# The second early expert slot: weights and x in two parts and three products, split while the first early slot runs

## The chip, the cores and the metric

The kernel runs on one core of one Trainium2 chip. The metric is device time in microseconds (us) of one execution. Inputs are laid out on the host before the launch; everything else is in the one launch that is timed.

## What is computed

The reference chains three parts (numbers: 3072 tokens of 384 features, from 4 batches, 768 steps, 8 heads of 48):

```python
# 1. linear attention with a decaying state
state = f[:, :, t, :, None] * state + einsum('bhd,bhe->bhde', k[:, :, t], v[:, :, t])
y[:, :, t] = einsum('bhd,bhde->bhe', q[:, :, t], state)
# 2. a mixture of 8 experts, one for each token, chosen by the largest logit
h = maximum(x[mask] @ w1[e], 0.0)          # 384 -> 1024
out[mask] = gate_w[mask, None] * (h @ w2[e])   # 1024 -> 384
# 3. a gated unit
out = (sigmoid(x @ w_gate) * (x @ w_val)) @ w_out   # 384 -> 1536 -> 384
```

The change lies in part 2.

## The kernel before, in words

**Stages.** Attention and routing run first, 24 token tiles of 128. Routing gives each token a place in its expert's list; a table of places, built by small matmuls from one-hot rows ("marks"), tells later which tokens an expert slot gathers. A slot is one expert's work on 256 gathered tokens. Two slots are "early": their experts and tokens are known from the first 18 tiles, so they can run while the tables for all other slots are still being made. After them come half slots (128 tokens; two run with these inputs), ten whole slots, and the gated unit, which takes over half of the time.

**A slot's steps.** A slot has eight steps f = 0 to 7, then f = 8 and 9. In a step TensorE makes 128 columns of h for the 256 tokens from three pieces of x and w1 (tile h, 128x256), ScalarE applies relu, and two steps later TensorE multiplies that h by w2 for two groups of 128 tokens (tile y, 128x384). Hooks hang on the steps: other work that is issued, in program order, right after a step's relu. Each engine takes its instructions in that order, so a hook's work on an engine stands ahead of all that the slot issues later on it.

**Two forms of a slot.** `slot32` (L688) keeps weights and x as fp32 and makes each product with one fp32 matmul: three for h (L704), one for each y (L694). VectorE has no part in it. `slot` (L646) holds weights and x as two fp32r parts, hi and lo, and makes three products: hi by hi, hi by lo, lo by hi (L656 to L659 for h, L735 for y). Its h needs the same: ScalarE writes relu(h) as hh (L662), and VectorE subtracts, max(h, 0) - hh, into hl (L663). `split` (L385) makes the parts of a weight piece of 128x1536: a ScalarE copy into hi (L388) and a subtraction into lo (L389), on VectorE or, if asked, on GpSimd. `transpose_x` (L399) turns gathered x with TensorE, copies it into xth with ScalarE (L405) and subtracts into xtl with VectorE (L406); `turn_x` (L723) only turns and copies it.

**The two early slots before.** Both are `slot32`. Their weights, `w0` and `w1`, four pieces each, are loaded together (L1350 to L1354, SyncE's queue). The first slot, `slot_0`, starts in the last attention round (L1284). Its hooks (L1402) are:

- f3: two loads of the weights of the gated unit, then six steps of the slot tables (`tab(6)`, VectorE, up to the expert numbers e_i, L546)
- f4: loads of the next expert's first weights, which wait for e_i; then five more steps of the tables, up to L580
- f5: `lates`, the marks of the last six tiles (VectorE, L307 and L309, six pairs)
- f6: `turn_x` for the second slot
- f7: a weight load
- f9, in the middle of the slot's last y products: `put_table` (L325), where TensorE puts the marks into the table (L331) and VectorE adds them (L334); a weight load

The second slot's hooks (L1429): at f0 `take_ids` (L341, TensorE reads the table; L343, VectorE), the gathers by GpSimd and one table step; f1 the rest of the tables; f2, f4, f5 VectorE work on the weights of the gated unit (`convert_high`, `convert_low`, L850 to L864) and, at f4 and f5, the split of `head`, the first piece of the next slot's weights (L1417, L1418); f8 and f9 `transpose_x` for the next slot. A branch (L1636) on the number of half slots follows it.

Of the kernel before, what the change touches and what calls it, by code (L numbers as in the profile page):

```python
# [45 lines left out]
STAGED = (3, 7)  # L46
# [14 lines left out]
def kernel(  # L61
# [16 lines left out]
    nc = tc.nc  # L78
# [10 lines left out]
    def ctile(shape, dtype, name):  # L89
        return const.tile(shape, dtype, name=name, tag=name)  # L90
# [42 lines left out]
    xth = ctile([P, 3, 256], F32R, "xth")  # L133
    xtl = ctile([P, 3, 256], F32R, "xtl")
    xg = ctile([P, 2, ROW], F32, "xg")
# [238 lines left out]
    st = {}  # L374

    def load_piece(e_reg, j, to=None):
        nc.sync.dma_start(out=raw[j] if to is None else to, in_=w12[bass.ds(e_reg, 1), j].rearrange("o p f -> (o p) f"))

    def alloc_w(pool, pre, j):
        return (  # L380
            pool.tile([P, 1536], F32R, name=f"{pre}h{j}", tag=f"{pre}h{j}"),
            pool.tile([P, 1536], F32R, name=f"{pre}l{j}", tag=f"{pre}l{j}"),
        )

    def split(dst, src, eng=None):  # L385

        hi, lo = dst
        nc.scalar.copy(out=hi, in_=src)  # L388
        (eng or nc.vector).tensor_tensor(out=lo, in0=src, in1=hi, op=ALU.subtract)  # L389
# [9 lines left out]
    def transpose_x(src, hi, lo, ts=(0, 1)):  # L399
        for t in ts:  # L400
            ps = ps_t.tile([P, 3, P], F32, tag="t", name="xT")
            for c in range(3):
                nc.tensor.transpose(ps[:, c, :], src[:, t, c * P:(c + 1) * P], ident)  # L403
            sl = slice(t * P, (t + 1) * P)
            nc.scalar.copy(out=hi[:, :, sl], in_=ps)  # L405
            nc.vector.tensor_tensor(out=lo[:, :, sl], in0=ps, in1=hi[:, :, sl], op=ALU.subtract)  # L406
# [222 lines left out]
    def run(steps):  # L629
        for _ in steps:  # L630
            pass

    def take_cur(src=None, ts=(0, 1)):
        cur = small.tile([P, 2, 2], F32, tag="cur", name="cur")
        sl = slice(0, len(ts))
        nc.gpsimd.tensor_copy(out=cur[:, sl], in_=xg[:, sl, DM:DM + 2] if src is None else src[:, sl])
        return cur
# [8 lines left out]
    def slot(w, hooks, src=None, last=False):  # L646

        cur = st.pop("cur") if "cur" in st else take_cur(src)
        yps = [ps_o.tile([P, DM], F32, tag="o", name=f"y{t}") for t in range(2)]
        hs = {}  # L650
        for f in range(9):
            if f < 8:
                hi, lo = (t.rearrange("p (c n f) -> p c n f", c=3, n=4)[:, :, f % 4, :] for t in w[f // 4])
                ps = ps_mm.tile([P, 256], F32, tag="mm", name="h")
                for c in range(3):
                    nc.tensor.matmul(out=ps, lhsT=hi[:, c, :], rhs=xth[:, c, :], start=(c == 0), stop=False)  # L656
                    nc.tensor.matmul(out=ps, lhsT=hi[:, c, :], rhs=xtl[:, c, :], start=False, stop=False)  # L657
                for c in range(3):
                    nc.tensor.matmul(out=ps, lhsT=lo[:, c, :], rhs=xth[:, c, :], start=False, stop=(c == 2))  # L659
                hh = hp["p"].tile([P, 256], F32R, tag="hh", name="hh", bufs=4)  # L660
                hl = hp["p"].tile([P, 256], F32R, tag="hl", name="hl", bufs=4)
                nc.scalar.activation(out=hh, in_=ps, func=AF.Relu)  # L662
                nc.vector.scalar_tensor_tensor(  # L663
                    out=hl, in0=ps, scalar=0.0, in1=hh, op0=ALU.max, op1=ALU.subtract
                )
                hs[f] = (hh, hl)
            for hook in hooks.get(f, ()):
                hook()
            if 2 <= f < 8:
                for t in range(2):  # L670
                    second_product(hs[f - 2], yps[t], w, f - 2, t)
            yield
        for t in range(2):
            for g in (6, 7):
                second_product(hs[g], yps[t], w, g, t)
            for hook in hooks.get(9, ()) if t == 0 else ():
                hook()
            ysb = hp["p"].tile([P, ROW], F32, tag="ysb", name="ysb", bufs=3)
            if t and last:
                nc.vector.tensor_scalar(  # L680
                    out=ysb[:, 0:DM], in0=yps[t], scalar1=cur[:, t, 0:1], scalar2=None, op0=ALU.mult
                )
            else:
                nc.scalar.activation(out=ysb[:, 0:DM], in_=yps[t], func=AF.Copy, scale=cur[:, t, 0:1])
            nc.gpsimd.tensor_copy(out=ysb[:, DM:ROW], in_=cur[:, t, :])
            st["y", t] = ysb

    def slot32(w, x, hooks, cur):  # L688

        yps = [ps_o.tile([P, DM], F32, tag="o", name=f"y{t}") for t in range(2)]  # L690
        hs = {}

        def second(g, t):
            nc.tensor.matmul(  # L694
                out=yps[t], lhsT=hs[g][:, t * P:(t + 1) * P], rhs=w[2 + g // 4][:, (g % 4) * DM:(g % 4 + 1) * DM],
                start=(g == 0), stop=(g == 7),
            )

        for f in range(9):
            if f < 8:  # L700
                piece = w[f // 4].rearrange("p (c n f) -> p c n f", c=3, n=4)[:, :, f % 4, :]
                ps = ps_mm.tile([P, 256], F32, tag="mm", name="h")
                for c in range(3):
                    nc.tensor.matmul(out=ps, lhsT=piece[:, c, :], rhs=x[:, c, :], start=(c == 0), stop=(c == 2))  # L704
                hs[f] = hp["p"].tile([P, 256], F32, tag="hh", name="h32", bufs=4)
                nc.scalar.activation(out=hs[f], in_=ps, func=AF.Relu)
            for hook in hooks.get(f, ()):
                hook()
            if 2 <= f < 8:
                for t in range(2):  # L710
                    second(f - 2, t)
            yield
        for t in range(2):
            for g in (6, 7):
                second(g, t)
            for hook in hooks.get(9, ()) if t == 0 else ():
                hook()
            ysb = hp["p"].tile([P, ROW], F32, tag="ysb", name="ysb", bufs=3)
            nc.scalar.activation(out=ysb[:, 0:DM], in_=yps[t], func=AF.Copy, scale=cur[:, t, 0:1])
            nc.gpsimd.tensor_copy(out=ysb[:, DM:ROW], in_=cur[:, t, :])  # L720
            st["y", t] = ysb

    def turn_x(x, ts=(0, 1)):  # L723

        for t in ts:
            ps = ps_t.tile([P, 3, P], F32, tag="t", name="xT")
            for c in range(3):
                nc.tensor.transpose(ps[:, c, :], xg[:, t, c * P:(c + 1) * P], ident)
            nc.scalar.copy(out=x[:, :, t * P:(t + 1) * P], in_=ps)
# [84 lines left out]
    stage = {}  # L814
# [415 lines left out]
    pools = {0: (wa, "a")}  # L1230
# [6 lines left out]
    early_x = [raw[2][:, 0:768].rearrange("p (c n) -> p c n", c=3)]  # L1237
    early_cur = []
# [6 lines left out]
    for i in range(NT + 2):  # L1245
# [103 lines left out]
        if i == NE + 2:  # L1349
            w0, w1 = ([wa.tile([P, 1536], F32, name=f"e{h}{j}", tag=f"a{h}{j}") for j in range(4)] for h in "hl")  # L1350
# [20 lines left out]
        stage[j] = staged.tile([P, 1536], F32, name=f"stage{j}", tag=f"stage{j}")  # L1371
    cv = ExitStack()
    hp["cv"] = cv.enter_context(tc.tile_pool(name="cv", bufs=1))
    early_x.append(stage[STAGED[-1]][:, 0:768].rearrange("p (c n) -> p c n", c=3))

    def each(hooks, **more):
        for f, fn in more.items():
            hooks.setdefault(int(f[1:]), []).extend(fn if isinstance(fn, list) else [fn])
        return hooks
# [7 lines left out]
    lates = late_marks()  # L1387

    def tab(n):
        for _ in range(n):  # L1390
            next(tables)
# [5 lines left out]
    def load_first():  # L1397
        st["e0"] = expert(0)
        for x in range(2):
            load_piece(st["e0"], x)  # L1400

    each(  # L1402
        hooks_0,
        f3=[convert_load, convert_load, lambda: tab(6)],
        f4=[load_first, lambda: tab(5)],
        f5=lambda: run(lates), f6=lambda: turn_x(early_x[1]),
        f7=lambda: load_piece(st["e0"], 2),
        f9=[put_table, lambda: load_piece(st["e0"], 3)],
    )
    run(slot_0)  # L1410
# [15 lines left out]
    def load_n():  # L1426
        st["n"] = nc.values_load(tabs["n"][0:1, 0:1], min_val=0, max_val=NHALF)

    run(slot32(w1, early_x[1], each(  # L1429
        {},  # L1430
        f0=[take_ids, lambda: gather_x(NTOK, 0), lambda: tab(1)],
        f1=[lambda: early_y.extend(scatter_y(tabs["edst"][:, 0])), lambda: run(tables)],
# [1 line left out]
        f4=[lambda: part(head, 0, 0), convert_mask, convert_high],  # L1434
        f5=[lambda: part(head, 0, 1), convert_low, convert_store],
        f7=load_n,
        f8=lambda: transpose_x(xg, xth, xtl, (0,)),
        f9=[lambda: transpose_x(xg, xth, xtl, (1,)), lambda: next_x((0, 1), (0, 1), 1)],
    ), early_cur[1]))
    scatter_y(tabs["edst"][:, 1], apart=early_y)  # L1440


# [324 lines left out]
```

## Time and profile before

| | |
|---|---|
| median of 3 runs | 879.07 us (875.2 to 879.09) |
| the profiled execution | 878.71 us |
| its span, first to last instruction | 877.0 us |
| granted TensorE clock, mean over the span | 0.991 |
| TensorE (PE) busy | 853.0 us, 97% |
| VectorE (DVE) busy | 476.8 us, 54% |
| ScalarE (ACT) busy | 389.2 us, 44% |
| GpSimd (POOL) busy | 249.8 us, 28% |

Times in the rows are in microseconds from the start of the span, durations in microseconds too unless marked ns. PE is TensorE, PEld its weight loads, DVE VectorE, ACT ScalarE, POOL GpSimd, SP SyncE; a "q" behind the name is the engine's sequencer. An fp32 matmul is recorded as two MATMUL records, so "x6" are three of them.

### The profile page before, as it was taken

What the parts mean: (1) busy time and instruction counts of PE and PEld (TensorE: products, weight loads), DVE (VectorE), ACT (ScalarE), POOL (GpSimd) and SP (SyncE); (2) the same over time, 40 slices, a digit from 0 to 9 for tenths busy, and PEclk for the clock granted to TensorE, in tenths of its full rate; (3) what the DMA queues carried; (4) which work ended last, traced back from release to release, by engine and by line L of the source; (5) the groups of instructions that cost most, each with busy time, mean ns of one, the idle gap of its engine ahead of it and who ended that gap; (6) DMA issues with size and microseconds to landing.
All of it is one profiled execution on the core that took longest, in us unless ns stands there. A gap on an engine that the chain in (4) does not pass through costs nothing.

```text
span 877.0 us, 15315 instructions
## 1 busy us (share of the span) xinstructions
PE 853.0 (97%) x5802; PEld 762.9 (87%) x5802; DVE 476.8 (54%) x1036; ACT 389.2 (44%) x804; POOL 249.8 (28%) x321
## 2 busy tenths in 40 slices
PE   7999999999999999999999999999999999999995
PEld 6888888777999999999888888888888888888885
DVE  5777778475987979976335334333423433442221
ACT  5866675225866656656432322232322332223222
POOL 5744443113445665564630200020020001002002
PEclk8999999999999999999999999999999999999998
DMA  9566653864989979976202021011012002000000
GB/s 324 177 219 232 217 171 123 332 242 149 336 302 327 330 270 321 333 260 226 80 10 64 27 47 35 1 55 37 18 46 46 19 1 64 10 0 37 1 1 36
DMA packets 52273, 121.15 MB, mean 138 GB/s; under 512 B 21018, under 2 KB 33318, under 8 KB 52192
## 3 DMA queue, kind: packets, MB, share of 16 engines
q1 hardware_dynamic: 47200, 105.10, 35.6%
q0 software_dynamic: 4992, 15.00, 4.8%
q8 instruction: 47, 0.77, 0.4%
q14 instruction: 34, 0.28, 0.1%
HBM read 96.44 MB, written 20.11 MB: 133 GB/s over the span
## 4 chain that ended last, share of the span: by engine, by line
PE 69%; DVE 4%; issue 1%; ACT 1%; POOL 0%; POOLq 0%; DVEq 0%; ACTq 0%
PE gv L1595 11%; PE gv L1596 11%; PE gv L1594 11%; PE y L735 8%; PE o L1619 6%; PE o L1617 6%; PE o L1618 6%; PE h L659 3%; PE h L656 3%; PE h L657 3%; DVE cvt L850 2%; DVE al L389 1%; DVE hl L663 1%; PE xT L403 0%; DVE bl L389 0%
## 5 line engine op out<-in xcount | busy, mean ns | idle before, releaser
L1605 DVE TENSOR_TENSOR sg<-sg,gv 128x256 f32<-128x256 f32 (+1 forms) x145 | 60.2, 415 | 209.3 <-PE gv L1596 209.3
L1606 ACT CAST gh<-sg 128x256 fp32r<-128x256 f32 (+1 forms) x145 | 58.7, 405 | 191.6 <-DVE sg L1605 191.6
L1625 POOL DMA_INDIRECT out_dram<-raw,tok x24 | 23.6, 984 | 375.5 <-ACT raw L1622 369.3
L1607 DVE TENSOR_TENSOR gl<-sg,gh 128x256 fp32r<-128x256 f32 (+1 forms) x145 | 64.3, 443 | 68.2 <-ACT gh L1606 68.2
L1604 ACT ACTIVATE sg<-gv 128x256 f32<-128x256 f32 (+1 forms) x145 | 55.2, 381 | 94.7 <-PE gv L1596 92.6
L393 POOL DMA_INDIRECT xg<-xd,ids x24 | 36.5, 1523 | 62.9 <-PE xT L403 38.9
L662 ACT ACTIVATE hh<-h 128x256 fp32r<-128x256 f32 x80 | 30.9, 386 | 42.7 <-PE h L659 42.0
L663 DVE SCALAR_TENSOR_TENSOR hl<-h,hh 128x256 fp32r<-128x256 f32 x80 | 33.3, 419 | 21.8 <-ACT hh L662 18.2
L1596 PE MATMUL gv<-oddh,al 128*128 128x512 f32 (+1 forms) x120 | 44.3, 369 | 0.0
L1595 PE MATMUL gv<-oddl,ah 128*128 128x512 f32 (+1 forms) x120 | 44.3, 369 | 0.0
L1594 PE MATMUL gv<-oddh,ah 128*128 128x512 f32 (+1 forms) x120 | 44.1, 367 | 0.0
L1596 PE MATMUL gv<-oddh,bl 128*128 128x512 f32 x108 | 42.5, 394 | 0.0
L1596 PE MATMUL gv<-evenh,bl 128*128 128x512 f32 x108 | 42.5, 393 | 0.0
L1595 PE MATMUL gv<-oddl,bh 128*128 128x512 f32 x108 | 42.4, 393 | 0.0
L1595 PE MATMUL gv<-evenl,bh 128*128 128x512 f32 x108 | 42.4, 393 | 0.0
L945 POOL TENSOR_TENSOR qT<-kq,g 128x512 f32<-128x512 f32 x19 | 24.4, 1283 | 62.9 <-ACT g L935 47.8
L1596 PE MATMUL gv<-evenh,al 128*128 128x512 f32 x108 | 42.3, 391 | 0.0
L1595 PE MATMUL gv<-evenl,ah 128*128 128x512 f32 x108 | 42.2, 391 | 0.0
L1594 PE MATMUL gv<-evenh,ah 128*128 128x512 f32 x108 | 42.0, 389 | 0.0
L1594 PE MATMUL gv<-evenh,bh 128*128 128x512 f32 x108 | 42.0, 389 | 0.0
L1594 PE MATMUL gv<-oddh,bh 128*128 128x512 f32 x108 | 42.0, 389 | 0.0
L975 DVE TENSOR_TENSOR am<-a,causal 128x512 f32<-128x512 f32 x48 | 31.2, 683 | 12.5 <-PE a L969 12.5
(365 smaller groups left out, 2487.8 us busy)
## 6 DMA issues: line engine op xcount, KB each, us to landing
raw<-in_w_dram SPq DMA_DIRECT2D x48, 768.0 KB, 5.8
kq<-in_att_kq_dram SPq DMA_DIRECT2D x24, 512.0 KB, 5.4
cvr<-in_w_glu_dram SPq DMA_DIRECT2D x14, 768.0 KB, 7.4
raw<-wd SPq DMA_DIRECT2D x7, 768.0 KB, 5.3
f<-in_att_fv_dram SPq DMA_DIRECT2D x24, 200.0 KB, 5.6
v<-in_att_fv_dram SPq DMA_DIRECT2D x24, 200.0 KB, 2.5
x<-yd SPq DMA_DIRECT2D x12, 386.0 KB, 3.4
xd<-rows SPq DMA_DIRECT2D x5, 772.0 KB
```

Of the source, the lines that this page charges most:

```text
L663: nc.vector.scalar_tensor_tensor(out=hl, in0=ps, scalar=0.0, in1=hh, op0=ALU.max, op1=ALU.subtract)
L735: nc.tensor.matmul(out=ps, lhsT=lhs[:, ts], rhs=rhs[:, fs], start=(g == 0 and part == 0), stop=(g == 7 and part == 2))
L1594: nc.tensor.matmul(out=ps[:, ns], lhsT=hi[:, sl], rhs=xh[:, c, ns], start=(c == 0), stop=False)
L1595: nc.tensor.matmul(out=ps[:, ns], lhsT=hi[:, sl], rhs=xl[:, c, ns], start=False, stop=False)
L1596: nc.tensor.matmul(out=ps[:, ns], lhsT=lo[:, sl], rhs=xh[:, c, ns], start=False, stop=(c == 2))
L1604: nc.scalar.activation(out=sg[:, sl], in_=pss[0][:, to], func=AF.Sigmoid)
L1605: nc.vector.tensor_tensor(out=sg[:, sl], in0=sg[:, sl], in1=pss[1][:, to], op=ALU.mult)
L1606: nc.scalar.copy(out=gh[:, sl], in_=sg[:, sl])
L1607: nc.vector.tensor_tensor(out=gl[:, sl], in0=sg[:, sl], in1=gh[:, sl], op=ALU.subtract)
L1617: nc.tensor.matmul(out=ps, lhsT=gh[:, ts], rhs=hi[:, fs], start=(f == 0), stop=False)
L1618: nc.tensor.matmul(out=ps, lhsT=gh[:, ts], rhs=lo[:, fs], start=False, stop=False)
L1619: nc.tensor.matmul(out=ps, lhsT=gl[:, ts], rhs=hi[:, fs], start=False, stop=(f == 11))
```

## The change

The second early slot becomes a `slot`. New tiles w1s, hi and lo of all four pieces of w1, lie in the pool of the odd slots' weights. They are made by `split` from hooks of the first slot: piece 0 at f3 and piece 2 at f4, with GpSimd subtracting, pieces 1 and 3 at f7 and f8, with VectorE subtracting. x of the second slot is made by `transpose_x` into xth and xtl at f6 in place of `turn_x`. The hooks of the second slot stay as they were.

```diff
-    early_x.append(stage[STAGED[-1]][:, 0:768].rearrange("p (c n) -> p c n", c=3))
...
+    w1s = [alloc_w(*pools[1], j) for j in range(4)]
+
+    def split_early(j, eng=None):
+        split(w1s[j], w1[j], eng)
+
     each(
         hooks_0,
-        f3=[convert_load, convert_load, lambda: tab(6)],
-        f4=[load_first, lambda: tab(5)],
-        f5=lambda: run(lates), f6=lambda: turn_x(early_x[1]),
-        f7=lambda: load_piece(st["e0"], 2),
+        f3=[convert_load, convert_load, lambda: split_early(0, nc.gpsimd), lambda: tab(6)],
+        f4=[load_first, lambda: split_early(2, nc.gpsimd), lambda: tab(5)],
+        f5=lambda: run(lates), f6=lambda: transpose_x(xg, xth, xtl),
+        f7=[lambda: load_piece(st["e0"], 2), lambda: split_early(1)],
+        f8=lambda: split_early(3),
         f9=[put_table, lambda: load_piece(st["e0"], 3)],
     )
     run(slot_0)
...
-    run(slot32(w1, early_x[1], each(
+    st["cur"] = early_cur[1]
+    run(slot(w1s, each(
         {},
         f0=[take_ids, lambda: gather_x(NTOK, 0), lambda: tab(1)],
...
-    ), early_cur[1]))
+    )))
     scatter_y(tabs["edst"][:, 1], apart=early_y)
```

## Rows read from the trace of the kernel before

**Rows 1.** The page's first part: busy time, share, instructions of each engine.

```profile
PE 853.0 (97%) x5802; PEld 762.9 (87%) x5802; DVE 476.8 (54%) x1036; ACT 389.2 (44%) x804; POOL 249.8 (28%) x321
```

**Rows 2.** Windows, second early slot (length; busy of PE, PEld, DVE, ACT, POOL).

```profile
188.98:212.02 23.04, 22.28 (x92) 16.21 (x90) 13.12 (x30) 8.73 (x17) 7.92 (x10) 1.00 0.35 117
```

**Rows 3.** Timeline, PE, from the end of the first early slot (start, duration).

```profile
187.96 1.51 PE L694 MATMUL y<-eh,h 128*128 128x384 f32 x4
...
190.60 0.55 PE L341 MATMUL take<-sel,table 96*128 96x52 f32 x4
...
212.02 0.39 PE L753 MATMUL h<-head,xth 128*128 128x256 f32 x1 [0.76 <-ACTq L1636]
```

**Rows 4.** Timeline, PE, one step of the second early slot (fp32).

```profile
196.22 1.45 PE L694 MATMUL y<-el,h 128*128 128x384 f32 x4
...
198.81 1.45 PE L694 MATMUL y<-el,h 128*128 128x384 f32 x4
```

**Rows 5.** Timeline, PE, one step of a later slot (three fp32r products).

```profile
296.34 0.34 PE L735 MATMUL y<-ah,hh 128*128 128x384 f32 x1
...
298.45 0.34 PE L735 MATMUL y<-ah,hh 128*128 128x384 f32 x1
```

**Rows 6.** By line: splits and xtl of later slots (ns: min/median/max).

```profile
L388 ACT CAST bh<-raw x22: 1463/1473/1491, 236.4 to 406.6; 128x1536 fp32r<-128x1536 f32 x22
L389 DVE TENSOR_TENSOR bl<-raw,bh x17: 1745/1747/1759, 237.9 to 408.1; 128x1536 fp32r<-128x1536 f32 x17
L389 POOL TENSOR_TENSOR bl<-raw,bh x5: 3499/3648/3696, 264.5 to 410.7; 128x1536 fp32r<-128x1536 f32 x5
L406 DVE TENSOR_TENSOR xtl<-xT,xth x23: 545/547/559, 208.9 to 398.7; 128x384 fp32r<-128x384 f32 x23
```

**Rows 7.** Timeline, DVE, in the two early slots.

```profile
175.08 0.25 DVE L506 TENSOR_REDUCE blocks<-fcmp 128x8 f32<-128x96 f32 x1
175.37 0.17 DVE L509 TENSOR_TENSOR blocks<-tiles,blocks 128x8 f32<-128x8 f32 x1
...
187.21 0.30 DVE L309 TENSOR_SCALAR raw<-iota_lo,late_lo,iota_t 128x128 f16<-128x128 bf16 x1
188.16 0.42 DVE L334 TENSOR_TENSOR table<-table,put 96x256 f32<-96x256 f32 x1 [0.65 <-PE put L331]
...
191.18 0.21 DVE L343 TENSOR_SCALAR ids<-take 128x52 int32<-128x52 f32 x1 [2.61 <-PE take L341]
```

**Rows 8.** Timeline, ACT, relus of steps 3 and 4 of the first early slot.

```profile
172.90 0.38 ACT L706 ACTIVATE h<-h 128x256 f32<-128x256 f32 x1 [2.67 <-PE h L704]
176.56 0.38 ACT L706 ACTIVATE h<-h 128x256 f32<-128x256 f32 x1 [3.27 <-PE h L704]
```

**Rows 9.** Timeline, SyncE's and POOL's queues in the two early slots.

```profile
181.22 7.26 SPq L377 DMA_DIRECT2D raw<-in_w_dram  x4
192.19 1.02 POOL L393 DMA_INDIRECT xg<-xd,ids  x1 [20.30 <-DVE skip L594]
```

**Rows 10.** Timeline, DVE and POOL at once, in three places.

```profile
143.70 1.33 DVE L309 TENSOR_SCALAR place<-iota_lo,lo,iota_t 128x128 f16<-128x128 bf16 x1
143.71 1.27 POOL L945 TENSOR_TENSOR qT<-kq,g 128x512 f32<-128x512 f32 x1 [4.75 <-ACT g L935]
...
251.19 3.52 POOL L389 TENSOR_TENSOR al<-raw,ah 128x1536 fp32r<-128x1536 f32 x1
251.72 4.61 DVE L389 TENSOR_TENSOR al<-raw,ah 128x1536 fp32r<-128x1536 f32 x1 [2.12 <-ACT ah L388]
...
264.45 3.50 POOL L389 TENSOR_TENSOR bl<-raw,bh 128x1536 fp32r<-128x1536 f32 x1 [4.25 <-ACT bh L388]
265.14 0.42 DVE L663 SCALAR_TENSOR_TENSOR hl<-h,hh 128x256 fp32r<-128x256 f32 x1 [0.50 <-ACT hh L662]
```

**Rows 11.** Timeline, PE, a wait in a later slot.

```profile
256.71 0.44 PE L735 MATMUL y<-ah,hl 128*128 128x384 f32 x1 [1.84 <-DVE hl L663]
```

**Rows 12.** Windows, just behind that wait (PE clock third from the end).

```profile
257.60:261.00 3.40, 3.40 (x16) 3.40 (x15) 3.37 (x6) 0.86 (x2) 2.43 (x3) 0.53 0.84 292
```

## Prediction

> **What bounds the kernel now.** I read the page first: TensorE is busy for 97% of the span [rows 1], so a change pays where it shortens TensorE's own work, and only while nothing else makes TensorE wait. Then the windows: in the second early slot TensorE works 22.28 of 23.04 us, VectorE 13.12 and ScalarE 8.73 [rows 2]. That slot is bound by TensorE, and its fp32 form asks nothing of VectorE. Then the timeline of TensorE around the seam: the first slot's last y products start at 187.96, behind `put_table`; `take_ids` runs at 190.60; the slot ends at 212.02 - 0.76 = 211.26, and after the branch the next slot starts at 212.02 [rows 3]. Last the timeline of VectorE: its tables and marks run with no gap worth naming until the last mark, 187.21 + 0.30 = 187.51, and it then waits 0.65 for TensorE before it adds the table at 188.16 [rows 7]. That row is the one to see: VectorE is less than a microsecond from being the bound at this place.
>
> **The change, part by part.**
>
> *Second slot, TensorE.* From one y to the next a step lasts 198.81 - 196.22 = 2.59 us in fp32 [rows 4] and 298.45 - 296.34 = 2.11 in three products [rows 5], about half of it h and half y. Eight steps save 8 x 0.48 = 3.8 us. This is all the change can gain.
>
> By the Trainium skill ("FP8 and Floating Point Precision", TensorE Precision Notes) a true fp32 product is four passes through the array; three products of one pass would then save a quarter. A quarter of 8 x 2.59 is an estimated 5.2 us, and the sum below would end 1.4 us lower; the rows show 19%, not 25%, and they decide.
>
> *ScalarE, first slot.* Four copies of 1.47 us [rows 6], and two of x that replace two. ScalarE waits 2.67 and 3.27 us for TensorE before the relus of steps 3 and 4 [rows 8], so I cost them at nothing. Without that cover a relu would be 1.47 late, and the y that needs it comes two steps later.
>
> *GpSimd, first slot.* Two subtractions of about 3.5 us [rows 6]. The first can start after relu and copy, 172.90 + 0.38 + 1.47 = 174.8; the second at 176.56 + 0.38 + 1.47 = 178.4 [rows 8], just as the first ends. Nothing that is urgent queues behind them: GpSimd idles 20.30 us before the gather at 192.19 [rows 9]. But VectorE works at the same time, and that has a price. A TENSOR_TENSOR on VectorE with both inputs in SBUF, 1.75 us alone [rows 6], took 4.61 beside a GpSimd subtraction and ended 1.6 us after it. A mark of L309, 0.30 alone [rows 7], took 1.33 and ended 0.05 us after a GpSimd multiplication. A hl of L663, which reads one input from PSUM, was not held at all, 0.42 [rows 10]. The tables and marks are nearly all of the first kinds. Bounds: nothing, if they behave as L663; 2 x 3.65 = 7.3 us if both subtractions hold VectorE throughout. It can't be a gain, since no work leaves VectorE here. I take 6.7: the two subtractions, 7.0, less the reduction (0.25) that can run under the first [rows 7]; the rows of the marks are the nearest, being the same instruction.
>
> [...]
>
> *SyncE.* The weight loads at 181.22 [rows 9] wait for the expert numbers that VectorE makes, and slide by the same 6.7 us, as do the two loads behind them in the queue. They are first wanted by a hook in the fifth step of the second slot, which slides too, so I cost this at nothing; the next loads start only behind the branch.
>
> *The put.* With the last mark at 187.51 + 6.7 = 194.2, TensorE, which stands at `put_table`, resumes its y at 187.96 + 6.7 = 194.7.
>
> *VectorE, end of the first slot.* Behind the marks come two xtl (2 x 0.55) and two subtractions (2 x 1.75) [rows 6], and only then, in program order, the addition to the table (0.42) [rows 7]: 194.2 + 1.1 + 3.5 + 0.4 = 199.2. TensorE is through its y (half a fp32 step, 1.3) and the first h (1.1) at 197.1 and waits 2.1 us at `take_ids`. Take starts at 199.3 in place of 190.60 [rows 3], 8.7 late.
>
> *VectorE, second slot.* Now each y needs a hl from VectorE, and the hl stand in its queue between the tables and the weight conversions. From the ids on, VectorE has its 13.12 us of the window [rows 2], less two xtl that come at the end (1.1), so 12.0, and seven hl of 0.42 [rows 10], 2.9: 14.9 us without a break. The ids start at 191.18 + 8.7 = 199.9 [rows 7], so the last hl is ready at 214.8. Behind it stand y of two h (one period, 2.1): the end is 216.9. TensorE alone would need from take on 0.4 + seven h and eight y (7 x 2.11 + 1.05) + two transpositions (0.7) = 16.9, ending at 216.2; VectorE ends last.
>
> *Sum.* 216.9 against 211.26 is 5.7 us later; everything after the branch shifts as one, since weights there are loaded step by step behind it. The profiled execution took 878.71 us, so 884.4. The median, 879.07, stands 0.36 above that execution: I say 884.6.
>
> **Rivals.**
>
> A, *the subtractions on GpSimd hold nothing up.* The place is VectorE between 174.8 and 182; it decides at a delay of some 5 us there. Marks end at 187.5, the table is added at 187.5 + 1.1 + 3.5 + 0.4 = 192.5, take is 2.0 late, and the same tail ends at 193.2 + 14.9 + 2.1 = 210.2: 1.0 us earlier, 877.7. For it: the row of hl, not held. Against it: the other two pairs of [rows 10], 4.61 for 1.75 and 1.33 for 0.30. Not slower; chance 0.17. [...]
>
> B, *the whole gain.* If VectorE's queue were free at both places, 3.8 us less: 874.9. Against it: the 0.65 us of idle time, to which 4.6 us of work is added ahead of the table. Chance 0.04.
>
> C, *half of it.* Only one subtraction meets work that it can hold (a copy that comes later, or loses its turn to VectorE): 3.4 us in place of 6.7, so 881.1. Chance 0.12.
>
> D, *TensorE's clock falls in the new wait.* TensorE would stand some 7 us at the put. In a later slot it waited 1.84 us [rows 11], and just behind that the granted clock was 0.53 for 3.4 us, near the lower level of 1.2 GHz [rows 12]: 1.6 us of work lost. In the forecast such a stretch is mostly covered, because TensorE has to wait 2.1 us at take anyway. Where it lasts past take, or comes twice, 1.6 to 3.2 us are added: 886.2 to 887.8. Chance 0.15.
>
> That the change doesn't do what it says is possible in one way: the splits spill out of the first slot. In the forecast two of the four do (until 198.8, beyond the old start of the second slot at 188.98 [rows 2]); that is priced.
>
> **How the numbers follow.** The forecast has 0.52, A 0.17, B 0.04, C 0.12, D 0.15. Half a per cent, 4.4 us, is about what a measurement of this kernel can tell from no change; the bounds are 874.7 and 883.5. The forecast lies 1.1 us above the upper bound and could be off by that much (6.4 or 7.3 us held, the tail a step shorter): I give 0.45 of its 0.52 to slower. With D that makes 0.60 slower; A, C and the rest 0.36 same; B 0.04 faster. The range runs from just under A (877.6) to D's upper end and a little noise, 888.3; it leaves out B, part of A's lower side and the far end of D.
>
> **What would show it.** In the changed profile: table operations of VectorE of 3 us and more where they took 0.2 before, at about 175 and 179; the last mark at about 194; a wait of TensorE of 6 to 7 us at L331, on VectorE; the table added near 199; a second, shorter wait of TensorE at L341; steps of 2.1 us in the second slot, broken by waits for hl at its end; the branch near 217.7. The forecast is wrong if the last mark stays before 190 (then A), if take is not late, or if y products of the second slot never wait for hl; and wrong in its first term if the steps there are not near 2.1 us.

## The result, and the profile after

The kernel with the change takes 882.92 us (median of 10 runs, 880.58 to 885.88) against 876.12 us for the kernel before beside it (10 runs, 875.12 to 879.56): 1.0062 times as long, 95% interval [1.0042, 1.0081]. It is slower by 3.7 to 7.1 us. The two medians alone would give 1.0078: nine of the ten runs of before lie near 875.3 or near 879.3 us, and the ratio is taken over all runs. The profiled execution took 883.42 us, 4.71 more than that of before.

The whole time scatters by about as much as the change moves: single runs of the kernel before lie between 874.79 and 880.94 us in the comparisons of this document, its medians between 876.12 and 878.85. And the copy of the token counts (VectorE, L370), from which the tables are made, stands between 171.51 and 175.84 in the profiled executions. So the stretch in question is measured by itself. I call it **the seam**: from the start of that copy to the first product behind the branch. In the kernel before the copy starts at 173.81 and the product at 212.02 [rows 3]: 38.21 us. After the change it is 216.75 - 172.96 = 43.79, which is 5.58 more. The copy stood 0.85 earlier in this execution; 5.58 - 0.85 = 4.73 is what the two executions differ by (4.71), so the rest of the program adds nothing in sum. The seam repeats well: in the table below the kernels before, e8 and e9 have 38.21, 38.22 and 38.22 us, and the pairs e6, e11 and e7, e10, which differ only in later slots, agree to 0.02.

The page's first part, after the change:

```profile
PE 853.9 (97%) x5842; PEld 767.5 (87%) x5842; DVE 487.5 (55%) x1048; ACT 394.1 (45%) x808; POOL 252.8 (29%) x323
```

VectorE gained 10.7 us of work [rows 1] in twelve more instructions. The timeline of VectorE in the two early slots (start, duration) shows where most of it is not work but time held:

```profile
172.96 0.17 DVE L370 COPY n_all<-cnt 128x8 f32<-128x8 f32 x1 [1.37 <-PE cnt L368]
...
176.07 3.47 DVE L485 TENSOR_SCALAR u<-ge,over 128x26 f32<-128x26 f32 x1
179.57 3.37 DVE L532 TENSOR_TENSOR u<-u,is_half 128x26 f32<-128x26 f32 x1
...
192.71 0.30 DVE L309 TENSOR_SCALAR raw<-iota_lo,late_lo,iota_t 128x128 f16<-128x128 bf16 x1
192.93 1.01 DVE L406 TENSOR_TENSOR xtl<-xT,xth 128x384 fp32r<-128x384 f32 x2
193.87 3.41 DVE L389 TENSOR_TENSOR bl<-el,bh 128x1536 fp32r<-128x1536 f32 x2
197.20 0.41 DVE L334 TENSOR_TENSOR table<-table,put 96x256 f32<-96x256 f32 x1
...
198.88 0.20 DVE L343 TENSOR_SCALAR ids<-take 128x52 int32<-128x52 f32 x1
...
212.97 0.75 DVE L663 SCALAR_TENSOR_TENSOR hl<-h,hh 128x256 fp32r<-128x256 f32 x2
```

The same two operations of 26 columns in the kernel before, from its timeline of VectorE:

```profile
176.92 0.29 DVE L485 TENSOR_SCALAR u<-ge,over 128x26 f32<-128x26 f32 x1
177.25 0.18 DVE L532 TENSOR_TENSOR u<-u,is_half 128x26 f32<-128x26 f32 x1
```

Over the same time, GpSimd's timeline after the change:

```profile
176.07 6.83 POOL L389 TENSOR_TENSOR bl<-el,bh 128x1536 fp32r<-128x1536 f32 x2 [6.40 <-DVE ge L485]
```

Each of the two small operations starts beside one subtraction and ends with it. Nothing else is held: from copy to the end of the last mark it is 193.01 - 172.96 = 20.05, against 187.51 - 173.81 = 13.70 before [rows 7]: 6.35 more, of which these two rows are (3.47 - 0.29) + (3.37 - 0.18) = 6.37. Then come xtl, two subtractions, and only behind them the addition to the table at L334, 4.2 us after the last mark.

The timeline of TensorE shows what that does at `put_table` and `take_ids`, and how the seam ends:

```profile
191.06 2.38 PE L331 MATMUL put<-raw 128*96 128x128 f16 x12 [4.45 <-DVE raw L309]
193.23 2.87 PE L694 MATMUL y<-eh,h 128*128 128x384 f32 x4
...
197.82 0.59 PE L341 MATMUL take<-sel,table 96*128 96x52 f32 x4
...
202.23 0.52 PE L659 MATMUL h<-xth,bl 128*128 128x256 f32 x3
...
204.35 0.52 PE L659 MATMUL h<-xth,bl 128*128 128x256 f32 x3
...
206.46 0.52 PE L659 MATMUL h<-xth,bl 128*128 128x256 f32 x3
...
207.38 0.44 PE L735 MATMUL y<-bh,hl 128*128 128x384 f32 x1 [0.23 <-DVE hl L663]
...
209.09 0.52 PE L659 MATMUL h<-xth,bl 128*128 128x256 f32 x3
...
213.44 0.44 PE L735 MATMUL y<-bh,hl 128*128 128x384 f32 x1 [0.16 <-DVE hl L663]
...
216.75 0.39 PE L753 MATMUL h<-head,xth 128*128 128x256 f32 x1 [0.77 <-ACTq L1642]
```

TensorE waits 4.45 us at the put, and longer inside it, where each pair of marks is waited for. A step of the second slot lasts 204.35 - 202.23 = 2.12, in place of 2.59 [rows 4]. The windows (length; busy of PE, PEld, DVE, ACT, POOL; granted clock third from the end) show one more thing, a stretch behind that wait at half clock, the lower of the two levels:

```profile
191.20:198.00 6.80, 6.65 (x27) 5.13 (x27) 6.41 (x14) 0.58 (x1) 0.00 (x0) 0.51 0.77 293
198.00:216.00 18.00, 17.59 (x122) 16.67 (x120) 15.69 (x38) 7.67 (x15) 7.11 (x8) 1.00 0.28 93
```

### The profile page after: what moved, and what is told of

It reads as the page before. It is cut to its first block, busy times and chain, and to the rows that moved or that the text cites. A ratio compares the mean times of both kernels' runs of the same rounds, so it can differ in the third digit from the quotient of the medians.

```text
span 881.7 us, 15420 instructions
## 1 busy us (share of the span) xinstructions
PE 853.9 (97%) x5842; PEld 767.5 (87%) x5842; DVE 487.5 (55%) x1048; ACT 394.1 (45%) x808; POOL 252.8 (29%) x323
## 4 chain that ended last, share of the span: by engine, by line
PE 67%; DVE 4%; DMA 1%; issue 1%; ACT 1%; POOL 0%; SPq 0%; POOLq 0%; DVEq 0%; ACTq 0%
PE gv L1601 11%; PE gv L1602 11%; PE gv L1600 11%; PE y L735 7%; PE o L1625 6%; PE o L1623 6%; PE o L1624 6%; PE h L659 3%; PE h L656 3%; PE h L657 2%; DVE cvt L850 2%; DMA cvr<-in_w_glu_dram 1%; DVE al L389 1%; DVE hl L663 1%; PE xT L403 0%
## 5 line engine op out<-in xcount | busy, mean ns | idle before, releaser
L662 ACT ACTIVATE hh<-h 128x256 fp32r<-128x256 f32 x88 | 33.9, 385 | 50.6 <-PE h L659 49.6
L663 DVE SCALAR_TENSOR_TENSOR hl<-h,hh 128x256 fp32r<-128x256 f32 x88 | 36.5, 418 | 22.8 <-ACT hh L662 22.4
```

The source lines that it names most:

```text
L663: nc.vector.scalar_tensor_tensor(out=hl, in0=ps, scalar=0.0, in1=hh, op0=ALU.max, op1=ALU.subtract)
```

## The experiments

The theory is that of the forecast: GpSimd's subtractions hold VectorE's tables (some 6 us), the rest of what VectorE got more to do eats most of the 3.8 us that TensorE saves. The rivals: GpSimd has no part in it and VectorE's own extra work, or three products themselves, make the slot long. Each row below is one profiled execution and its comparison with the kernel before.

| run | seam, us | against before | median, us | ratio, 95% interval |
|---|---|---|---|---|
| before | 38.21 | | | |
| the change | 43.79 | +5.58 | 882.92 | 1.0062 [1.0042, 1.0081] |
| e1 no GpSimd | 37.89 | -0.32 | 878.4 | 1.0002 [0.9981, 1.0023] |
| e2 no lo | 35.42 | -2.79 | 875.63 | 0.9966 [0.995, 0.9982] |
| e3 all on VectorE | 40.51 | +2.30 | 880.18 | 1.0019 [0.9997, 1.0041] |
| e4 unused splits | 47.04 | +8.83 | 886.86 | 1.0098 [1.0065, 1.0132] |
| e5 table first | 40.02 | +1.81 | 879.7 | 1.0023 [1.0006, 1.0039] |
| e6 light queue | 34.87 | -3.34 | 876.75 | 0.9977 [0.9964, 0.9989] |
| e7 half in three | 36.87 | -1.34 | 876.59 | 0.9977 [0.9963, 0.9991] |
| e8 only moved | 38.22 | +0.01 | 880.56 | 1.002 [1.0008, 1.0032] |
| e9 later hook | 38.22 | +0.01 | 877.16 | 0.9976 [0.996, 0.9993] |
| e10 half in three, later hook | 36.85 | -1.36 | 875.39 | 0.9963 [0.9947, 0.9979] |
| e11 light queue, later hook | 34.88 | -3.33 | 875.0 | 0.9965 [0.9948, 0.9982] |

**Is it GpSimd?** e1 leaves out GpSimd's two subtractions; hi is used in the place of lo, so TensorE and ScalarE have the same work:

```diff
+    for j in (0, 2):
+        w1s[j] = (w1s[j][0], w1s[j][0])
     def split_early(j, eng=None):
-        split(w1s[j], w1[j], eng)
+        if j in (0, 2):
+            nc.scalar.copy(out=w1s[j][0], in_=w1[j])
+        else:
+            split(w1s[j], w1[j], eng)
```

> Left out: the lo parts of pieces 0 and 2 (hi is read in their place), so GpSimd subtracts nothing and TensorE's work stays. Measure: the seam, from the copy of the counts (L370) to the first product behind the branch; it was 38.2 us before and is 43.8 with the change. Theory (GpSimd's two subtractions hold VectorE for 6.7 us): the marks end as early as before, the table is added about 4 us late because of xtl and two subtractions on VectorE, and the seam is 37.2 us, a little below before. Rival (the holding costs nothing, VectorE's added work is all): the seam stays within 1 us of 43.8.

The seam is 37.89, 5.90 less than with them. VectorE's timeline in e1:

```profile
171.51 0.17 DVE L370 COPY n_all<-cnt 128x8 f32<-128x8 f32 x1 [1.36 <-PE cnt L368]
174.95 0.19 DVE L532 TENSOR_TENSOR u<-u,is_half 128x26 f32<-128x26 f32 x1
...
184.91 0.31 DVE L309 TENSOR_SCALAR raw<-iota_lo,late_lo,iota_t 128x128 f16<-128x128 bf16 x1
```

L532 is back at 0.19, and the last mark ends 13.71 behind the copy, as before. The rival falls. The seam is 0.7 longer than expected: VectorE's two subtractions make TensorE wait 1.68 us at take, and behind that wait its granted clock is 0.50 for 3.4 us, as a window of e1 shows:

```profile
191.40:194.80 3.40, 3.40 (x17) 3.40 (x16) 2.83 (x13) 1.39 (x3) 2.62 (x3) 0.50 0.26 66
```

The whole time comes out level with before, which is also what the seam says (-0.32).

e4 asks the reverse: the kernel before, with only the two hi copies and GpSimd's two subtractions added, and nothing reading them.

```diff
+    w1s = [alloc_w(*pools[1], j) for j in range(4)]
+    def split_early(j, eng=None):
+        split(w1s[j], w1[j], eng)
...
-        f3=[convert_load, convert_load, lambda: tab(6)],
-        f4=[load_first, lambda: tab(5)],
+        f3=[convert_load, convert_load, lambda: split_early(0, nc.gpsimd), lambda: tab(6)],
+        f4=[load_first, lambda: split_early(2, nc.gpsimd), lambda: tab(5)],
```

> The kernel before, with the change's first two splits (ScalarE copy, GpSimd subtraction) added at the same hooks and their results not used. Both early slots stay in fp32, so VectorE's queue matters only up to the table. Theory: the marks end 6.7 us late, TensorE waits for them at the put, and nothing later covers it: seam 44.8 us, or up to 46.8 if TensorE's clock falls in that wait and the fp32 slot runs into the low stretch. Rival (GpSimd holds nothing up): seam 38.2.

VectorE and GpSimd in e4:

```profile
174.10 0.17 DVE L370 COPY n_all<-cnt 128x8 f32<-128x8 f32 x1 [1.36 <-PE cnt L368]
...
177.08 3.43 DVE L485 TENSOR_SCALAR is_half<-sv,over 128x26 f32<-128x26 f32 x1
180.42 3.48 DVE L485 TENSOR_SCALAR u<-ge,over 128x26 f32<-128x26 f32 x1
...
193.92 0.31 DVE L309 TENSOR_SCALAR raw<-iota_lo,late_lo,iota_t 128x128 f16<-128x128 bf16 x1
```

```profile
177.00 6.87 POOL L389 TENSOR_TENSOR bl<-el,bh 128x1536 fp32r<-128x1536 f32 x2 [6.32 <-SPq L1088]
```

The marks end 20.13 behind the copy, 6.43 later than in the kernel before, and the seam grows by 8.83. GpSimd's work, on an engine that had been idle for 20.30 us there [rows 9], makes the kernel 1% slower by itself. (Two ScalarE copies came with it; e1 has these too, and there the marks end as before.) The 2.4 us beyond the hold come between the marks and the ids. TensorE's timeline and a window of e4 show them:

```profile
192.27 2.38 PE L331 MATMUL put<-raw 128*96 128x128 f16 x12 [4.53 <-DVE raw L309]
199.68 0.58 PE L341 MATMUL take<-sel,table 96*128 96x52 f32 x4
```

```profile
193.00:199.80 6.80, 6.63 (x20) 4.69 (x19) 1.65 (x8) 0.58 (x1) 0.00 (x0) 0.50 0.69 254
```

From the end of the marks to take it is 199.68 - 194.23 = 5.45 us, against 190.60 - 187.51 = 3.09 before [rows 3, 7]: TensorE was granted half its clock behind the wait, and in this kernel VectorE's table had long been ready, so that loss is laid bare. The expected 44.8 to 46.8 had allowed for most of it.

**What do VectorE's own additions cost?** e2 leaves out all four subtractions (hi in place of lo for all pieces; the diff is that of e1 with `(0, 1, 2, 3)`).

> Left out: the lo parts of all four pieces (hi is read in their place). TensorE's work stays, VectorE keeps xtl, hl, tables and conversions. Theory: take is no more than 0.5 us late, then VectorE's queue in the second slot (14.9 us from the ids to the last hl, and 2.1 of products) ends the slot, seam 35.0 us. Rival (VectorE's queue in the second slot hides behind TensorE): the whole saving of 3.8 us shows, seam 34.4 or less.

35.42: VectorE's two subtractions ahead of the table were worth 37.89 - 35.42 = 2.47 us of seam. Of these 1.83 are take's later start (18.40 us behind the copy in e1, 16.57 in e2); the rest lies behind take, where e1 has its slow stretch and e2 has none. Without any subtraction the change would be a gain, 0.9966, and in the seam 2.8 of the 3.8 us. The 35.42 is nearer the theory's 35.0 than the rival's 34.4, and in e2 two y still wait for hl (0.22 and 0.19 us). e3 keeps the result whole and lets VectorE make all four, the first two behind the table steps of their hooks:

```diff
-        f3=[convert_load, convert_load, lambda: split_early(0, nc.gpsimd), lambda: tab(6)],
-        f4=[load_first, lambda: split_early(2, nc.gpsimd), lambda: tab(5)],
+        f3=[convert_load, convert_load, lambda: tab(6), lambda: split_early(0)],
+        f4=[load_first, lambda: tab(5), lambda: split_early(2)],
```

> All four lo parts made by VectorE, pieces 0 and 2 behind the table steps of their hooks; the result is the same. VectorE gets 3.4 us more work and loses 6.7 us of being held. Theory: marks end 3.4 us late in place of 5.3 to 6.7, the table is added 3.4 us earlier than with the change, seam 40.3 us (3.4 below the change). Rival (what counts is the amount of work on VectorE, not the holding): 3.4 us more work, seam 47 us.

VectorE in e3:

```profile
173.07 0.17 DVE L370 COPY n_all<-cnt 128x8 f32<-128x8 f32 x1 [1.36 <-PE cnt L368]
...
189.82 0.31 DVE L309 TENSOR_SCALAR raw<-iota_lo,late_lo,iota_t 128x128 f16<-128x128 bf16 x1
```

40.51, and the marks 3.36 later than before: two subtractions of 1.75 done by VectorE delay it by half of what it loses when GpSimd does them for it. The work that was handed to GpSimd cost VectorE more than doing it. e5 goes on from e3 and puts the other two behind the addition to the table:

```diff
-        f7=[lambda: load_piece(st["e0"], 2), lambda: split_early(1)],
-        f8=lambda: split_early(3),
-        f9=[put_table, lambda: load_piece(st["e0"], 3)],
+        f7=lambda: load_piece(st["e0"], 2),
+        f9=[put_table, lambda: split_early(1), lambda: split_early(3), lambda: load_piece(st["e0"], 3)],
```

> On the run with all four lo parts made by VectorE (seam 40.5 us): the splits of pieces 1 and 3 move behind the table's addition, in the same hook. VectorE does the same work in another order. Theory (VectorE is without a break from the marks to the last hl, so the amount of work ends the slot): take comes 2 us and more earlier, hl later waits longer, seam 39.8 to 40.2 us. Rival (the wait at take is what costs): the 2.0 us of that wait are gained, seam 38.5.

40.02, 0.5 less than e3, though the table is ready 3 us sooner. TensorE and VectorE in e5:

```profile
188.09 2.28 PE L331 MATMUL put<-raw 128*96 128x128 f16 x12 [1.44 <-DVE raw L309]
...
194.15 0.61 PE L341 MATMUL take<-sel,table 96*128 96x52 f32 x4
```

```profile
190.90 0.40 DVE L334 TENSOR_TENSOR table<-table,put 96x256 f32<-96x256 f32 x1
191.22 3.41 DVE L389 TENSOR_TENSOR bl<-el,bh 128x1536 fp32r<-128x1536 f32 x2
```

Take stands 2.8 us behind the table: what it waits for is TensorE's own late y and first h, and these ran at half clock. The same window in e5 and then in e3 (granted clock third from the end):

```profile
190.80:194.20 3.40, 3.40 (x13) 2.64 (x12) 3.40 (x4) 0.58 (x1) 0.00 (x0) 0.51 0.69 231
```

```profile
190.80:194.20 3.40, 2.06 (x13) 1.46 (x11) 3.40 (x3) 0.96 (x2) 0.00 (x0) 1.00 0.72 228
```

An earlier take would have gained little all the same. The ids stand in VectorE's queue behind both subtractions in either order, and start 22.20 us behind the copy in e5, 22.41 in e3. From the marks to the last hl VectorE has gaps of 0.22 us in all in e5 and of 0.76 in e3, and that difference is about the half microsecond gained. So the theory held: moving VectorE's work within the seam gains little as long as its amount, ahead of the last hl, ends the slot.

**Can the change be made to pay?** e6 puts no split ahead of the marks: all four on VectorE, at f7 and f9 of the first slot and f1 and f3 of the second; and it takes the two weight conversions of the second slot to slots 12 and 15.

```diff
-TWICE = (13, 14, 16, 17, 18)
+TWICE = (12, 13, 14, 15, 16, 17, 18)
...
-        f3=[convert_load, convert_load, lambda: split_early(0, nc.gpsimd), lambda: tab(6)],
-        f4=[load_first, lambda: split_early(2, nc.gpsimd), lambda: tab(5)],
+        f3=lambda: tab(6),
+        f4=[load_first, lambda: tab(5)],
...
-        f7=[lambda: load_piece(st["e0"], 2), lambda: split_early(1)],
-        f8=lambda: split_early(3),
-        f9=[put_table, lambda: load_piece(st["e0"], 3)],
+        f7=[lambda: load_piece(st["e0"], 2), lambda: split_early(0)],
+        f9=[put_table, lambda: split_early(2), lambda: load_piece(st["e0"], 3)],
...
-        f1=[lambda: early_y.extend(scatter_y(tabs["edst"][:, 0])), lambda: run(tables)],
-        f2=[convert_mask, convert_high, convert_low, convert_store],
-        f4=[lambda: part(head, 0, 0), convert_mask, convert_high],
-        f5=[lambda: part(head, 0, 1), convert_low, convert_store],
+        f1=[lambda: early_y.extend(scatter_y(tabs["edst"][:, 0])), lambda: split_early(1)],
+        f2=lambda: run(tables),
+        f3=lambda: split_early(3),
+        f4=lambda: part(head, 0, 0),
+        f5=lambda: part(head, 0, 1),
```

> VectorE makes all lo parts, each just ahead of the step that needs it (piece 0 behind the marks, 2 behind the table, 1 and 3 in the second slot), and the two weight conversions of the second slot (6.9 us of VectorE) move to two later whole slots. The result is the same. Theory (the saving of 3.8 us is there once VectorE's queue is short enough): no wait of note for VectorE, seam 34.7 us, 3.5 below before; whole time 2 to 3 us below before, since each later slot that takes a conversion pays 0.3 to 0.8. Rival (three products don't save 3.8 us here, or the moved conversions cost as much as they free): the time of before or above.

34.87: with VectorE out of the way 3.34 of the 3.8 us appear. In e6 it is VectorE that waits for the last hl, and TensorE for nothing of it. VectorE in e6:

```profile
202.41 0.42 DVE L663 SCALAR_TENSOR_TENSOR hl<-h,hh 128x256 fp32r<-128x256 f32 x1 [0.88 <-ACT hh L662]
```

But the whole gains about 2 us, not 3.3. e8 is the kernel before with nothing but the two conversions moved (the TWICE line of e6, the two loads of f3 and the hooks of f2, f4 and f5 removed).

> The kernel before, with only the two weight conversions moved from the second early slot to two later whole slots, as in the run with the light queue. Theory: the seam stays at 38.2 us, since the fp32 slot never waits for VectorE; the whole time is 0.6 to 1.6 us longer, by the two later slots. Rival (VectorE's load in the second early slot costs something already): the seam shrinks by 0.5 us or more.

Its seam is as before and it is 1.7 us slower (1.002): that is what e6 pays elsewhere. e7 leaves the conversions where they were and takes half the change: h in three products, y in fp32. That needs no hl and only two splits, both on VectorE.

```diff
     # slot32, h of one step, with w = w1s and x = None
+    hi, lo = (t.rearrange("p (c n f) -> p c n f", c=3, n=4)[:, :, f % 4, :] for t in w[f // 4])
+    for c in range(3):
+        nc.tensor.matmul(out=ps, lhsT=hi[:, c, :], rhs=xth[:, c, :], start=(c == 0), stop=False)
+        nc.tensor.matmul(out=ps, lhsT=hi[:, c, :], rhs=xtl[:, c, :], start=False, stop=False)
+    for c in range(3):
+        nc.tensor.matmul(out=ps, lhsT=lo[:, c, :], rhs=xth[:, c, :], start=False, stop=(c == 2))
...
+    w1s = [alloc_w(*pools[1], j) for j in range(2)] + w1[2:]
...
+        f7=[lambda: load_piece(st["e0"], 2), lambda: split_early(0)],
...
+        f1=[lambda: early_y.extend(scatter_y(tabs["edst"][:, 0])), lambda: split_early(1), lambda: run(tables)],
```

> Only h of the second slot is made in three products (pieces 0 and 1 and x split, lo by VectorE, none by GpSimd); y stays one fp32 product, so no hl is needed and the conversions stay. The result is the same. Theory: half of the saving, 1.8 us, without VectorE on the way to any y, seam 36.5 us; whole time 1.5 to 2 us below before. Rival (the saving lies in y rather than h, or VectorE's two splits ahead of take cost as much): seam 38 us or more.

36.87, with this step (TensorE's timeline of e7):

```profile
198.33 1.46 PE L694 MATMUL y<-el,h 128*128 128x384 f32 x4
...
200.70 1.46 PE L694 MATMUL y<-el,h 128*128 128x384 f32 x4
```

2.37 us, midway between 2.59 and 2.11 [rows 4, 5]. Half of the saving and hardly any of the price: 0.9977, as much as e6.

**The same hold in later slots.** Why did two moved conversions cost 1.7 us? In the slots of TWICE the conversion at f5 starts beside GpSimd's subtraction of f4. One of them in the kernel before, VectorE, GpSimd and TensorE:

```profile
283.08 3.02 DVE L850 TENSOR_SCALAR cvt<-cvr 128x768 int32<-128x768 int32 x1
...
289.48 0.44 PE L735 MATMUL y<-bh,hl 128*128 128x384 f32 x1 [0.58 <-DVE hl L663]
```

```profile
282.04 3.64 POOL L389 TENSOR_TENSOR al<-raw,ah 128x1536 fp32r<-128x1536 f32 x1 [6.02 <-ACT ah L388]
```

The conversion takes 0.55 us alone (201.08, in the second early slot of the kernel before). In e8 the two moved conversions meet a subtraction as well and take 2.91 and 3.11 us. The view of TensorE's waits from 220 to 425 us (us in total, times, longest), for the kernel before and then for e8, accounts for 1.3 of the 1.7 us:

```profile
PE y L735 <- DVE hl L663: 4.9, 6, 1.8
```

```profile
PE y L735 <- DVE hl L663: 6.2, 8, 1.8
```

The last three runs move that hook by one step: e9 in the kernel before, e10 in e7, e11 in e6.

```diff
-            each(hooks, f5=[convert_mask, convert_high], f8=[convert_low, convert_store])
+            each(hooks, f6=[convert_mask, convert_high], f8=[convert_low, convert_store])
```

> The kernel before with one hook of five later slots moved by a step: in the slots where the conversion of the gated unit's weights (L850) is issued at f5, just beside GpSimd's subtraction of f4, it takes 3.02 to 3.09 us in place of 0.55, and a y product behind it then waits 0.58, 0.62, 0.57, 0.64 and 0.62 us for hl; here it is issued at f6. Theory (GpSimd's subtraction holds VectorE's operations of this kind wherever they meet, and what is queued behind them pays): those five waits go, 3.0 us less than before, 0.9965. Rival (VectorE has just enough time in these slots, so the later conversion makes a hl or xtl late at the slot's end instead): the waits turn up later in the slot, no change.

> The form with h in three products and y in fp32, no hl and only two splits, both on VectorE (0.9977 when run with the conversions where they were, 2 us less than before), with the same hook of the later slots at f6. Theory: the two gains add, 2.0 + 3.0 = 5.0 us less than before, 0.994. Rival: no gain from the hook, 0.9977.

> The form with all three products in the second early slot, all subtractions on VectorE just ahead of need and two conversions moved to later slots (0.9977 when run with the later slots' hook at f5), with that hook at f6 in all seven slots that have it. Theory: the two conversions that were moved cost 1.7 us because they met GpSimd's subtraction too; with seven waits of 0.6 us gone, 4.2 us less than that form: 2.0 + 4.2 = 6.2 us less than before, 0.993. Rival: the later conversion crowds VectorE in seven slots, 0.998 or above.

The same slot in e9, and the view of TensorE's waits over these five slots, 276 to 382 us, for e9 and then for the kernel before:

```profile
285.70 0.92 DVE L850 TENSOR_SCALAR cvt<-cvr 128x768 int32<-128x768 int32 x1
...
289.69 0.45 PE L735 MATMUL y<-bh,hl 128*128 128x384 f32 x1 [0.26 <-DVE hl L663]
```

```profile
PE y L735 <- DVE hl L663: 1.5, 5, 0.3
```

```profile
PE y L735 <- DVE hl L663: 3.0, 5, 0.6
```

The hold is gone but for its last third of a microsecond, and half of the wait with it: 1.5 us, and the whole gained 1.7 (0.9976). The other half stays, since conversion and subtraction now stand together ahead of the next hl. Theory and rival were each right in part. e10 came out at 875.39 us against 878.82 (0.9963 [0.9947, 0.9979]), e11 at 875.0 (0.9965 [0.9948, 0.9982]): over 3 us faster than before, less than the 5.0 and 6.2 expected, because the hook gave half of what I had reckoned with: in e11 the waits for hl from 220 to 425 us come to 5.0 us against 7.1 in e6, where 4.2 less was expected, and the conversion of slot 12 still meets a subtraction (2.05 us). These two beat the kernel before, and the change, whose interval lies above 1; which of them is better the intervals don't tell.

## Why the prediction was right

The forecast was 5.7 us more than before, by a mechanism in four steps. The execution showed 5.58 in the seam, and the ratio lies at 5.4 us (0.62% of 876.12). The 884.6 forecast for the median met 882.92, inside the range. Step by step:

- **TensorE's saving**, 8 x 0.48 = 3.8: steps of 2.12 measured, and 3.34 of the 3.8 appeared in e6 once VectorE was out of the way. By the rule of four passes that I weighed against this ("FP8 and Floating Point Precision", TensorE Precision Notes, of the Trainium skill) a quarter would have gone; a step fell by 18%. In the forecast's own sum, where VectorE ends the slot, that quarter would not have brought the end forward by the 1.4 us that I wrote, but by an estimated 0.2, the shorter last period (1.94 for 2.11). Where the rest of the quarter went, TensorE's rows show: half of a fp32 step, 1.29 us, is three matmuls of h, 0.43 each, while the fp32r products of h start 0.12 us apart, so that three of them take 0.36, or 84%.
- **The hold**, 6.7: 6.35 measured at the last mark, 6.43 in e4 with nothing else changed but two ScalarE copies, none in e1. The bounds, nothing and 7.3, were far apart, and the row of the marks under a GpSimd multiplication [rows 10] was the right one to go by. Operations of 26 columns were held for all of a subtraction, 3.47 and 3.37 us. Rivals A and C fall with this.
- **The put and the table.** TensorE waited 4.45 us ahead of the put, and the put, paced by the marks, took 2.17 us to y in place of 0.67: 5.95 lost in all, for the 6 to 7 named. y resumed at 193.23, where 194.7 was forecast, 193.85 after the 0.85 us by which this execution was early; the table was added at 197.20, where 199.2 - 0.85 = 198.35 less the 0.4 of the addition itself, 197.9, was forecast.
- **The wait at take** did not come as I wrote it. I had 2.1 us of idle time there; TensorE was busy right up to take at 197.82. What came is the slow stretch of rival D: clock 0.51 for 6.8 us, y in 2.87 in place of 1.51 [rows 3]. I had said that such a stretch would be covered by the wait at take, and it was: TensorE at half clock came to take (197.82) just when the table was ready (197.20 + 0.41 = 197.61). That the two came out even is luck: nothing in the sum set the length of the stretch, and e4, where no such cover is, lost 2.4 us to one of the same length.
- **The tail.** From take the slot was to last 216.9 - 199.3 = 17.6; it lasted 215.98 - 197.82 = 18.16. The hl chain was right, 198.88 to 213.72 = 14.84 for the forecast's 14.9. The 0.56 lies at both ends of it: the ids came 1.06 behind take's start, 0.46 later than I had them, since a hl that waits for ScalarE stands ahead of them, and y behind the last hl took 2.26 for 2.1. It made up for take being 0.63 early. That the end fit to 0.07 us is luck too: two errors of 0.6 us cancel.
- **Covers.** ScalarE's copies cost the first slot nothing, as costed: its last y before the put start at 183.87, as in the kernel before (184.71) less the 0.85. No wait for SyncE's loads shows in the seam. One hi copy started 2.06 us late, for a reason that the trace doesn't settle; the first subtraction began at 176.07 instead of 174.8, and the hold was the same.

That y would wait for hl at the slot's end was right in kind and small: 0.23 and 0.16 us of idle time. The step with the first of these waits lasts 209.09 - 206.46 = 2.63 us for 2.12, so I estimate that the two cost about 1 us together. By no more than that did VectorE, and not TensorE, end the slot (0.7 in the forecast, 216.9 against 216.2).

## What to carry to other kernels

Before work is given to an idle GpSimd, look at what VectorE does at that hour: a long GpSimd instruction can cost VectorE, by small instructions that it holds, more than doing the work itself would (6.35 us against 3.36 here). A saving on the engine that bounds the kernel is had only as far as the engines that now feed it keep up, so put their new work just ahead of its need, behind whatever the next stage waits for; and half of a change that needs no new chain (e7) can be worth as much as the whole. When an effect is found at one place, look for the same pair of rows elsewhere: moving one hook in five other slots gained about as much as either repaired form of the change (0.9976 and 0.9977).

## What was not expected of the hardware

A VectorE operation with one SBUF tile as input is held too. L850 reads one tile and two constants, and took 3.02 us beside GpSimd's 3.64. L485 of the tables reads one tile, and as scalars one or two single columns of another; it is one of the two operations held in the change and both of those held in e4. "SBUF — State Buffer" (Who interferes with whom) of the Trainium skill counts a VectorE instruction with at most one SBUF input as free of contention with GpSimd only outside the two-port modes. The trace fits that: L850 alone needs 0.55 us for 768 columns, while L853, over as many with two inputs, needs 0.96. That L850 runs in such a mode is read from these durations and not shown; no run here takes it out of one.

The loss behind TensorE's wait was larger than [rows 12] had suggested: 6.8 us at a clock of 0.50 or 0.51 behind 4.5 us of waiting, in the change and in e4, against 3.4 us behind a wait of 1.84 [rows 11]. And not every wait has one behind it: e5, which waited 1.44 us at the put, has 3.4 us at 0.51, while e3 waited 1.45 there and 1.96 more at take, and its granted clock is 1.00 from 184 to 214 us.
